# Attention and a Sinkhorn-routed MoE on one core: one plain unit more among the last four, and an earlier clear and cast in the first batch

## The chip, the core and the metric

The kernel runs on one core of one Trainium2 chip. A core has five engines that run their own instruction queues in order: TensorE (PE, matrix products; weight loads are shown apart as PEld), VectorE (DVE), ScalarE (ACT), GpSimd (POOL) and SyncE (SP), and 16 DMA engines that move data between HBM and the on-chip memory. Transfers are issued from the queues of SP, ACT and POOL. The metric is device time in microseconds (us) of one execution; lower is better.

## The reference

The program is an attention layer followed by a mixture of experts.

```python
# attention: 8 batches, 8 heads, 512 local and 32 global tokens, head dim 64
k_all = np.concatenate([k_g, k_l], axis=2); v_all = np.concatenate([v_g, v_l], axis=2)
out_g = np.matmul(sm(scale * q_g @ k_all.T), v_all)          # global queries see all keys
s_ll  = np.where(abs(i - j) <= 32, scale * q_l @ k_l.T, -1e9) # local queries: a band
s_l   = np.concatenate([scale * q_l @ k_g.T, s_ll], axis=-1)  # and all 32 global keys
out_l = np.matmul(sm(s_l), np.concatenate([v_g, v_l], axis=2))
# mixture of experts: x is 4352 tokens x 512, 8 experts, hidden size 1024
P = np.exp(x @ w_gate - max); 8 times: rows and columns of P normalised (Sinkhorn)
for e in range(8):
    out += P[:, e:e+1] * (np.maximum(x @ w1[e], 0) @ w2[e])
```

`sm` is the softmax. All inputs are float32; the kernel computes matrix products in float16 with float32 accumulation.

## The kernel before

**Stages.** From 0 to about 305 us the attention runs, one head pair per step `s` (32 steps, `hp` is the pair within a batch `b`), with matmuls of experts 0 and 1 put between its steps from step 5 on. From about 323 to 352 us the Sinkhorn iterations run, with matmuls of those two experts around and between them. From 357 us to the end experts 2 to 7 run, in two passes over halves of the tokens, by Strassen's scheme with seven products in place of eight: the first layer in slots of 512 columns (`Slot`), the second layer in units of two 128-token tiles (`Unit`). The order of all engines' instructions is the order in which the code writes them; each engine takes its own in that order.

**The first batch.** GpSimd's queue, in the order written, holds: q and k of heads 2 and 3 of batch 0 (`steps[0:2]`), the mask's four selects (L310), q and k of heads 4 to 7 (`steps[2:4]`, L174), then `load_v(0)`. Its `first()` issues `cast_vg(0)` (L183: the global values of the batch, cast to float16 into a scratch tensor in HBM) and the first local load of `va` (L193, 96 rows); three whole loads of `va` (L196) and one of `vb` (L200) follow. Then come `cast_vg(1)` and `clear_z(0)` (L296 to L301). That last function sets the padded tile `vgz` of the global values to zero, writes the column of ones (`own`) and clears the small tile `vgn`. SP's queue has `load_vz(0)` next (L180: four copies from the scratch into every fourth partition of `vgz`) and one copy into `vgn` (L319).

In step 1 GpSimd issues q and k of batch 1 and makes `vb` by copying from `va` (`part`, L204 to L209). `st_E` (L423) multiplies the probabilities with `va`, `vb` and `vgz`; it first runs in step 2. `st_A` (L332) transposes the q and k of a head pair; the pair with heads 4 and 5 is taken in step 1. VectorE's L427 and L428 read what `st_E` wrote.

**A Strassen unit.** `sums` forms three sums of quarters of the hidden activations (and overwrites one quarter) with four `tensor_tensor` operations, L867, on VectorE or on the engine passed to it. Seven products follow, each of four matmuls of 256 columns (L871), into an accumulator `z` of four quarters in PSUM (the pool has two of them): m1, then a copy on ScalarE (L885), m7, m2, m6 with another copy (L892), m4, m5, and m3. VectorE reads the results and adds them, weighted, to the output (L905): `r2` and `r7` after m5, `r1` after m3. In the last expert `r7` and `r1` are followed by a store on SP (L833).

**A plain unit.** `plain` (L931) does the same unit without the scheme: two tiles, each with eight matmuls of 512 columns (L940), in PSUM buffers of their own (pools `ps_mm` and `ps_sc`, two buffers each), read by VectorE at L943. Its argument `between` puts other pieces of work before given matmuls: the key (1, 3) means tile 1, before its matmul 3. With `last` the second tile is cut into 256, 128 and 128 columns. It reads the raw quarters of the activations, so it needs no `sums`.

**The end.** After the last slot (`p`) and the last unit of the regular order (`x`), four units are left, u0 to u3. u0 and u3 are plain, u1 and u2 are Strassen units; u2's sums are formed by GpSimd, and the two units' products are interleaved.

Of the kernel before, what the change touches and what calls it, by code (L numbers as in the profile page):

```python
# [23 lines left out]
def kernel(  # L24
# [13 lines left out]
    nc = tc.nc  # L38
# [14 lines left out]
    FT = F // P  # L53
# [75 lines left out]
    with ExitStack() as att:  # L129
# [22 lines left out]
        def natural(b):  # L152
            return b < 2
# [18 lines left out]
        def load_qk(b, *hs):  # L172
            staged[b] = tuple(att_in.tile([P, H, NJ, Dh], FP16, tag=t, name=t) for t in ("qs", "ks"))
            return [lambda t=t, src=src, h0=h0, h1=h1: nc.gpsimd.dma_start(  # L174
                        out=t[:, h0:h1], in_=src[b, h0:h1].rearrange("h (p s) d -> p h s d", s=NJ))
                    for h0, h1 in zip(hs, hs[1:]) for t, src in zip(staged[b], (q_l, k_l))]

        def load_vz(b):
            for i in range(4):
                nc.sync.dma_start(out=vgz[b % 2][i:P:4, i, :, 0:Dh], in_=vg16[b])  # L180

        def cast_vg(b):
            nc.gpsimd.dma_start(out=vg16[b], in_=v_g[b].rearrange("h g d -> g h d"))  # L183

        def load_v(b):
            va, vb = vab[b % 2]
            vz = vgz[b % 2]
            src = v_l[b].rearrange("h s d -> s h d")

            def first():  # L190
                if b != 1:
                    cast_vg(b)
                nc.gpsimd.dma_start(out=va[W:P, 0, :, 0:Dh], in_=src[0:96])  # L193

            def mid(j):
                nc.gpsimd.dma_start(out=va[:, j, :, 0:Dh], in_=src[P * j - W : P * j + 96])  # L196

            def last():
                r = HB if natural(b) else W
                nc.gpsimd.dma_start(out=vb[r : r + W, NJ - 1, :, 0:Dh], in_=src[Sl - W : Sl])  # L200

            def part(eng, lo):
                if lo:
                    eng.tensor_copy(out=vb[96:P, NJ - 1], in_=va[W : 2 * W, 0])  # L204
                    eng.tensor_copy(out=vb[0:HB, 0:2], in_=va[HB:P, 0:2])
                    eng.tensor_copy(out=vb[0:HB, 2:NJ], in_=va[HB:P, 2:NJ])
                else:
                    eng.tensor_copy(out=vb[HB:P, 0:2], in_=va[0:HB, 1:3])
                    eng.tensor_copy(out=vb[HB:P, 2], in_=va[0:HB, 3])  # L209

            def move():
                if natural(b):
                    return part
                nc.sync.dma_start(out=vb[96:P, NJ - 1], in_=va[W : 2 * W, 0])
                nc.sync.dma_start(out=vb[0:W, :], in_=va[HB : HB + W, :])
                nc.sync.dma_start(out=vb[HB : HB + W, :], in_=va[HB + W : P, :])
                nc.sync.dma_start(out=vb[W:HB, 0 : NJ - 1], in_=va[0:W, 1:NJ])
                nc.sync.dma_start(out=vb[HB + W : P, 0 : NJ - 1], in_=va[W:HB, 1:NJ])
                load_vz(b)

            return [first] + [lambda j=j: mid(j) for j in range(1, NJ)] + [last, move]
# [38 lines left out]
        def run(steps):  # L260
            for f in steps:
                f()
# [14 lines left out]
        steps = load_qk(0, 2, 4, H)  # L277
# [18 lines left out]
        def clear_z(i, eng):  # L296
            eng.memset(vgr[i].bitcast(mybir.dt.uint32), 0)
            eng.tensor_copy(out=vgz[i][:, :, :, Dh], in_=own.unsqueeze(2).to_broadcast([P, 4, H]))
            if i == 0:
                eng.memset(vgn[0 : P - Sg], 0.0)  # L300
                eng.memset(vgn[P - Sg : P, :, Dh:VW], 1.0)  # L301
# [5 lines left out]
        for a in range(2):  # L307
            band = mask[HB * a : HB * (a + 1), 1, 0:KW]
            for base, m, c in ((0, -1, 1), (2 * W, 1, -1)):
                nc.gpsimd.affine_select(out=band, in_=band, compare_op=ALU.is_ge, fill=NEG, base=base,  # L310
                                        pattern=[[c, KW]], channel_multiplier=m)
        run(steps[2:4])
        *steps, move = load_v(0)
        part = move()
        run(steps)
        cast_vg(1)
        clear_z(0, nc.gpsimd)
        load_vz(0)
        nc.sync.dma_start(out=vgn[P - Sg : P, :, 0:Dh], in_=vg16[0])  # L319

        st = {}
# [248 lines left out]
        for s in range(NU + 2):  # L570
            b, hp = divmod(s, HP)
# [189 lines left out]
    with tc.tile_pool(name="tpool", bufs=2) as tpool, \  # L761
# [68 lines left out]
        def store(m, c, eng):  # L830
            if m < B:
                r0 = S * m + Sg + P * c
                eng.dma_start(out=out[r0 : r0 + P, :], in_=ogs[m][:, c, :])  # L833
            else:
                for b in range(4 * c, 4 * c + 4):
                    eng.dma_start(out=out[S * b : S * b + Sg, :], in_=ogs[m][W * (b % 4) : W * (b % 4 + 1), c, :])
# [15 lines left out]
        class Unit:  # L852
# [6 lines left out]
            def o(self, j):  # L859
                return acc_of(self.m)[:, self.c[j], :]  # L860

            def sums(self, eng=nc.vector):
                a11, a12, a21, a22 = self.a
                s = self.s = hsum.tile([P, 3, HF, P], FP16, tag="hs", name="hs")
                for o, x, y, op in ((s[:, 1], a11, a21, ALU.subtract), (a21, a21, a22, ALU.add),
                                    (s[:, 0], a21, a11, ALU.subtract), (s[:, 2], a12, s[:, 0], ALU.subtract)):
                    eng.tensor_tensor(out=o, in0=x, in1=y, op=op)  # L867

            def mm(self, o, lhs, rhs, first):
                for fk in range(HF):  # L870
# [3 lines left out]
            def w(self, i, j):  # L874
                return w2s[self.k][:, HF * i : HF * (i + 1), H2 * j : H2 * (j + 1)]
# [55 lines left out]
        def plain(u, last, between):  # L931
            order = sorted(range(FT), key=lambda fk: (fk % HF == HF - 1, fk))
            for j in range(2):
                for d0, d1 in ((0, H2), (H2, 3 * P), (3 * P, D)) if last and j else ((0, D),):
                    pool, tag = (ps_sc, "sc") if (j + (d0 > 0)) % 2 else (ps_mm, "mm")
                    z = pool.tile([P, D], FP32, tag=tag, name="zp")
                    for n, fk in enumerate(order):
                        for f in between.get((j, n), ()) if d0 == 0 else ():
                            f()
                        nc.tensor.matmul(z[:, d0:d1], u.a[2 * j + fk // HF][:, fk % HF, :], work["last"][:, fk, d0:d1],  # L940
                                         start=(n == 0), stop=(n == FT - 1), skip_group_check=True)
                    o = u.o(j)[:, d0:d1]
                    nc.vector.scalar_tensor_tensor(out=o, in0=z[:, d0:d1], scalar=u.p[j], in1=o, op0=ALU.mult, op1=ALU.add)  # L943
                store(u.m, u.c[j], nc.sync)
# [171 lines left out]
        p, x = state["slot"], state["unit"]  # L1116
        for w in (x.m4, x.m5, x.r2, x.r7, p.m4, p.m3):
            w()
        u0, u1, u2, u3 = final
        u1.sums()  # L1120
        plain(u0, False, {(0, FT - 2): (x.m3, x.r1, lambda: u2.sums(nc.gpsimd)), (1, 3): (u1.m1,)})
        for w in (u1.m7, u1.m2, u1.m6, u2.m1, u1.m4, u1.m5, u1.r2, u1.r7, u2.m7, u2.m2, u2.m6, u1.m3, u1.r1):
            w()
        plain(u3, True, {(0, 3): (u2.m4, u2.m5, u2.r2, u2.r7), (0, FT - 2): (u2.m3, u2.r1)})


# [28 lines left out]
```

## Time and profile before

| | |
|---|---|
| median of 3 runs | 996.84 us (996.23 to 996.92) |
| profiled execution | 996.39 us, of which the span from the first to the last instruction is 994.6 |
| granted TensorE clock, mean | 0.998 |
| busy: PE, DVE, ACT, POOL | 98%, 78%, 66%, 31% of the span |
| HBM read, written | 144.46 MB, 39.58 MB |

The profile is of one execution. A row gives the start and the length in us, the engine, the line of the code, the operation and the tiles (written <- read). What stands in brackets is the idle time of the engine just before and what ended it. A row with a `q` behind the engine's name (SPq) is that of its queue. Rows of groups give the number of instructions (x4), the busy time in us, the mean of one in ns, and the idle time before them with what ended it. "The chain of waits" follows the work that ended last back to the start: at each step to what released it, or to the instruction before it on its engine. Matmuls are pipelined: the next starts before the last one's end, so two starts lie closer than one is long.

### The profile page before, as it was taken

The numbers are of one execution on the slowest core, as the hardware profiler recorded it, in microseconds if no ns is written. First come the engines' busy times: TensorE is split into PE (matmuls) and PEld (weight loads), VectorE is DVE, ScalarE is ACT, GpSimd is POOL, SyncE is SP. The second block draws the span as 40 slices with busy tenths as digits, with TensorE's granted clock in tenths as the row PEclk, the third lists the DMA queues.
The fourth block names the chain that finished last, engine by engine and source line by source line (L and its number), as shares of the span: only waits on it lengthen the run. The fifth ranks groups of instructions, "written<-read, shape, count | busy, mean of one in ns | idle before, by whom it ended". The sixth has DMA issues, their size and how long they took to land.

```text
span 994.6 us, 22109 instructions
## 1 busy us (share of the span) xinstructions
PE 978.8 (98%) x8644; PEld 637.0 (64%) x8644; DVE 776.9 (78%) x1919; ACT 659.8 (66%) x1372; POOL 305.2 (31%) x366
## 2 busy tenths in 40 slices
PE   7899999999999999999999999999999999999997
PEld 5565556555555556666666666676767676766765
DVE  7876666666663755899999888997899999888887
ACT  6898888888884566765555555557765555555551
POOL 9649887887860201111111111101111111100001
PEclk9999999999999999999999999999999999999999
DMA  9999999999952477554443333575654543123043
GB/s 165 189 163 207 226 213 212 224 203 234 225 141 85 121 229 189 161 138 118 117 106 75 75 74 75 138 212 138 160 138 118 117 116 71 38 56 73 2 106 128
DMA packets 138248, 138.65 MB, mean 139 GB/s; under 512 B 56800, under 2 KB 110240, under 8 KB 136096
## 3 DMA queue, kind: packets, MB, share of 16 engines
q0 software_dynamic: 105696, 87.32, 51.6%
q1 hardware_dynamic: 31888, 49.60, 15.7%
q8 instruction: 67, 1.10, 0.4%
q10 hardware_dynamic: 560, 0.33, 0.1%
q14 instruction: 37, 0.30, 0.1%
HBM read 144.46 MB, written 39.58 MB: 185 GB/s over the span
## 4 chain that ended last, share of the span: by engine, by line
PE 93%; DVE 2%; ACT 2%; POOL 1%; DMA 1%; issue 1%; SPq 0%; ACTq 0%; DVEq 0%; POOLq 0%
PE z L871 30%; PE pa L969 18%; PE py L537 12%; PE ph L523 11%; PE pb L969 9%; PE pc L969 4%; PE sc L375 1%; PE po L423 1%; PE ptw L389 1%; ACT Pu L382 1%; PE pk L332 1%; DMA vgz<-vg 1%; PE tgx L399 1%; PE pq L332 1%; PE sg L455 0%
## 5 line engine op out<-in xcount | busy, mean ns | idle before, releaser
L871 PEld LDWEIGHTS <-hs 128*128 128x128 f16 x2320 | 226.1, 98 | 96.1 <-issue 2.9
L871 PE MATMUL z<-w2e,hs 128*128 128x256 f16 x1336 | 200.4, 273 | 2.3 <-DVE o L905 1.0
L871 PE MATMUL z<-v,hs 128*128 128x256 f16 x984 | 147.6, 273 | 0.0
L892 ACT COPY z<-z 128x256 f32<-128x256 f32 x100 | 35.7, 357 | 145.9 <-PE z L871 145.9
L523 PE MATMUL ph<-xT,w1e 128*128 128x512 f16 (+1 forms) x576 | 130.2, 367 | 0.6 <-ACT xT L407 0.6
L537 PE MATMUL py<-w2e,hT 128*128 128x512 f16 x544 | 128.2, 379 | 0.0
L382 ACT ACTIVATE Pu<-ms,mx 128x160 f16<-128x160 f32 x256 | 119.6, 637 | 11.7 <-DVE mx L379 9.6
L969 PEld LDWEIGHTS <-w1e 128*128 128x128 f16 x960 | 87.1, 98 | 51.6 <-issue 1.0
L969 PE MATMUL pa<-t,s 128*128 128x512 f16 x384 | 114.2, 379 | 0.0
L787 POOL DMA_DIRECT2D w1e<-in_moe_w_dram x24 | 17.4, 733 | 290.7 <-PE pa L969 220.4
L379 DVE CUSTOM_DVE_ANT_0 ms<-sc,mask 128x160 f32<-128x160 f32 x256 | 70.0, 320 | 46.3 <-ACT yst L540 27.6
L867 DVE TENSOR_TENSOR hs<-hs 128x512 f16<-128x512 f16 x228 | 99.1, 435 | 8.4
L905 DVE SCALAR_TENSOR_TENSOR oy<-z,lg,oy 128x512 f32<-128x512 f32 x128 | 95.8, 748 | 7.3 <-ACT oy L910 5.9
L787 POOL DMA_DIRECT2D w2e<-in_moe_w_dram x24 | 19.8, 830 | 243.6 <-PE z L871 214.2
L973 DVE CUSTOM_DVE_ANT_0 hx<-pb,s 128x512 f16<-128x512 f32 x96 | 65.9, 686 | 36.4 <-ACT s L1003 30.4
L523 PEld LDWEIGHTS <-w1e 128*128 128x128 f16 x576 | 54.5, 98 | 53.0 <-issue 1.1
L989 ACT ACTIVATE hs<-pa 128x512 f16<-128x512 f32 x96 | 57.2, 596 | 46.8 <-PE pa L969 46.8
L973 DVE CUSTOM_DVE_ANT_0 hs<-pb,s 128x512 f16<-128x512 f32 x96 | 65.8, 686 | 24.1 <-ACT s L1003 23.7
L969 PEld LDWEIGHTS <-s 128*128 128x128 f16 x720 | 65.6, 98 | 28.5 <-issue 0.3
L537 PEld LDWEIGHTS <-hT 128*128 128x128 f16 x544 | 49.9, 98 | 51.9
L528 DVE TENSOR_SCALAR hT<-ph 128x512 f16<-128x512 f32 x58 | 40.1, 691 | 50.1 <-PE ph L523 50.0
L526 ACT ACTIVATE hT<-ph 128x512 f16<-128x512 f32 (+1 forms) x86 | 50.7, 589 | 27.6 <-PE ph L523 27.1
(203 smaller groups left out, 1935.0 us busy)
## 6 DMA issues: line engine op xcount, KB each, us to landing
ys<-yd SPq DMA_DIRECT2D x68, 256.0 KB, 3.2
yd<-yst SPq DMA_DIRECT2D x16, 1024.0 KB, 6.4
pw<-in_moe_w_dram POOLq DMA_DIRECT2D x24, 512.0 KB, 10.1
kept<-psum POOLq DMA_DIRECT2D x24, 512.0 KB, 4.8
s<-kept POOLq DMA_DIRECT2D x12, 768.0 KB, 8.8
v<-kept POOLq DMA_DIRECT2D x12, 768.0 KB, 8.7
w1e<-in_moe_w_dram POOLq DMA_DIRECT2D x12, 512.0 KB, 5.4
w2e<-in_moe_w_dram POOLq DMA_DIRECT2D x12, 512.0 KB, 6.5
```

What stands on the lines that cost most here:

```text
L379: nc.vector.tensor_tensor_reduce(out=ms[:, ii, :], in0=sc[:, SW * ii : SW * (ii + 1)], in1=mask[:, mi, :], scale=-scale, scalar=BIG, op0=A ...
L382: nc.scalar.activation(out=d["Pu"][:, i // 4, :, i % 4], in_=ms[:, ii, :], func=AF.Exp, scale=-1.0, bias=d["mx"][:, i : i + 1])
L523: nc.tensor.matmul(ph[:, 0:n], wts[e][0][:, dk, P * fm : P * (fm + 1)], xT[:, dk, c0 : c0 + n], start=(dk == 0), stop=(dk == DP - 1))
L526: nc.scalar.activation(out=hT[:, fm, 0:n], in_=ph[:, 0:n], func=AF.Relu)
L528: nc.vector.tensor_scalar(out=hT[:, fm, 0:n], in0=ph[:, 0:n], scalar1=0.0, scalar2=None, op0=ALU.max)
L537: nc.tensor.matmul(py, hT[:, fk, P * c : P * (c + 1)], wts[e][1][:, fk, :], start=(fk == 0), stop=(fk == FT - 1))
L867: eng.tensor_tensor(out=o, in0=x, in1=y, op=op)
L871: nc.tensor.matmul(o, lhs[:, fk, :], rhs[:, fk, :], start=(first and fk == 0), stop=(fk == HF - 1), skip_group_check=True)
L905: nc.vector.scalar_tensor_tensor(out=o, in0=z, scalar=p, in1=o, op0=ALU.mult, op1=ALU.add)
L969: nc.tensor.matmul(o, lhs[:, dk, P * f : P * (f + 1)], rhs[:, dk], start=(first and n == 0 and dk == 0), stop=(dk == HD - 1), skip_group_c ...
L973: nc.vector._custom_dve(TENSOR_ADD_SAT, out=self.to(i, j), in0=self.of(ps), in1=self.of(s), s0=BIG, s1=0.0)
L989: nc.scalar.activation(out=self.to(1, 0), in_=self.of(self.pa), func=AF.Relu)
```

## The change

Two places. At the start the cast of the first batch's global values, `cast_vg(0)`, is issued ahead of the second q/k pair (`steps[2:4]`) instead of inside `first()`; `clear_z(0)` stands behind the first local load instead of behind all loads and `cast_vg(1)`; and `load_vz(0)` is written behind the loads, ahead of `cast_vg(1)`. At the end u2 becomes a plain unit. It no longer has sums (`sums` loses its argument for the engine), u1's later products and reads stand between u2's matmuls, and u3 has nothing between its own.

```diff
             def first():
-                if b != 1:
+                if b > 1:
                     cast_vg(b)
                 nc.gpsimd.dma_start(out=va[W:P, 0, :, 0:Dh], in_=src[0:96])
...
+        cast_vg(0)
         run(steps[2:4])
         *steps, move = load_v(0)
         part = move()
-        run(steps)
+        steps[0]()
+        clear_z(0, nc.gpsimd)
+        run(steps[1:])
+        load_vz(0)
         cast_vg(1)
-        clear_z(0, nc.gpsimd)
-        load_vz(0)
         nc.sync.dma_start(out=vgn[P - Sg : P, :, 0:Dh], in_=vg16[0])
...
-            def sums(self, eng=nc.vector):
+            def sums(self):
...
-                    eng.tensor_tensor(out=o, in0=x, in1=y, op=op)
+                    nc.vector.tensor_tensor(out=o, in0=x, in1=y, op=op)
...
         u1.sums()
-        plain(u0, False, {(0, FT - 2): (x.m3, x.r1, lambda: u2.sums(nc.gpsimd)), (1, 3): (u1.m1,)})
-        for w in (u1.m7, u1.m2, u1.m6, u2.m1, u1.m4, u1.m5, u1.r2, u1.r7, u2.m7, u2.m2, u2.m6, u1.m3, u1.r1):
+        plain(u0, False, {(0, FT - 2): (x.m3, x.r1), (1, 3): (u1.m1,)})
+        for w in (u1.m7, u1.m2, u1.m6):
             w()
-        plain(u3, True, {(0, 3): (u2.m4, u2.m5, u2.r2, u2.r7), (0, FT - 2): (u2.m3, u2.r1)})
+        plain(u2, False, {(0, 3): (u1.m4, u1.m5, u1.r2, u1.r7), (1, 3): (u1.m3, u1.r1)})
+        plain(u3, True, {})
```

## The prediction

> **What bounds the kernel now.** First the page, for the engine on which the chain of waits ends.
>
> ```profile
> PE 93%; DVE 2%; ACT 2%; POOL 1%; DMA 1%; issue 1%; SPq 0%; ACTq 0%; DVEq 0%; POOLq 0%
> ```
>
> TensorE (PE) holds 93% of the chain, so the middle of the kernel has no room. What can be won lies where the chain leaves PE: in the first 22 us and the last 20. There I read the chain piece by piece (start, length, what). At the start:
>
> ```profile
> 11.27 0.97 POOL vgz L297
> 13.31 0.60 SPq L180
> 13.96 0.61 SPq L180
> 14.61 6.71 DMA vgz<-vg
> ```
>
> GpSimd (POOL) issues all its loads, only then clears the padded tile (from L297 on); SP then issues four copies into it, one after another, and the fourth lands at 14.61 + 6.71 = 21.32. PE's rows in order of time say what that costs:
>
> ```profile
> 20.53 0.19 PE L423 MATMUL po<-vgz,pg 128*64 128x65 f16 x1
> 21.36 0.19 PE L423 MATMUL po<-vgz,pg 128*64 128x65 f16 x1 [0.64 <-DMA vgz<-vg]
> ```
>
> Between the two starts lie 0.83 us, and without the wait some 0.03: a stall of 0.8. Now the end: the longest pieces of the chain, then the groups of the last 21 us.
>
> ```profile
> 980.95 0.67 DVE oy L905
> ...
> 983.96 0.76 DVE ox L905
> ...
> 987.70 0.76 DVE o L905
> ```
>
> ```profile
> L871 PE MATMUL z<-w2e,hs 128*128 128x256 f16 x36 | 5.4, 272 | 2.3 <-DVE o L905 1.0 <-DVE oy L905 1.0 <-DVE ox L905 0.3
> L867 POOL TENSOR_TENSOR hs<-hs 128x512 f16<-128x512 f16 x4 | 4.8, 1196 | 29.5 <-DVE hs L867 29.2
> L867 DVE TENSOR_TENSOR hs<-hs 128x512 f16<-128x512 f16 x4 | 4.3, 1070 | 0.2
> ```
>
> PE waits three times for VectorE (DVE): 1.0, 0.3 and 1.0 us. First: u2's m1 needs the accumulator that x.r1 empties (the piece at 980.95), and x.r1 stands in VectorE's queue behind u1's four sums, which take 1070 ns each while GpSimd forms u2's. Second and third: m3 of u1 goes on when r7 of u1 has ended (983.96 + 0.76 = 984.72), m3 of u2 when r7 of u2 has (988.46). With two Strassen units side by side there is too little other PE work between a unit's m5 and its m3.
>
> **The change, part one: the end.** On PE u2's 28 matmuls of 256 columns go and 16 of 512 come. Prices from unbroken pieces of the chain:
>
> ```profile
> 971.27 1.31 PE z L871 x12
> ...
> 985.36 0.65 PE zp L940 x3
> ```
>
> 28 x 1.31 / 12 = 3.06 us against 16 x 0.65 / 3 = 3.47: PE gets 0.41 more work.
>
> The waits that go: 2.3 us idle in the group's row above. Each restart also lays bare the tail of the matmul before it (272 ns long, started 109 apart: 0.16), three times 0.16 = 0.49. Together 2.8.
>
> What is late next? I lay the new order on the old clock. Up to u1.m6 PE's order is the old one. m6's last matmul ends at about 980.7 (the copy below starts on it), so PE's next turn is 0.16 earlier, 980.54. Then: three matmuls of plain(u2), to 981.19; m4 and m5 of u1, 0.44 each, to 982.06; eight of plain(u2), to 983.78; m3; five more, to 985.30; plain(u3). m4 writes what ScalarE's copy after m6 reads:
>
> ```profile
> 980.73 0.36 ACT L892 COPY z<-z 128x256 f32<-128x256 f32 x1 [2.03 <-PE z L871]
> ```
>
> That ends at 981.09, 0.1 ahead of m4's turn. r2 can begin some 0.2 us after m5 (its matmuls' tail and the semaphore), 982.26; r2 and r7 take 0.76 each and 0.03 between them, to about 983.80, so m3, due at 983.78, may wait 0.07. VectorE gets there in time, because the sums alone take
>
> ```profile
> L867 DVE TENSOR_TENSOR hs<-hs x1: 426/426/426, 971.7 to 971.7; 128x512 f16<-128x512 f16 x1
> ```
>
> 0.43 each: begun at 976.5 they end near 978.3, x.r1 and plain(u0)'s two reads follow by 980.5, and the rest (r2, r7, r1, three reads of 0.75, three shorter ones) is 5.7 us of work for 9 us of PE. The sums that GpSimd loses (4.8 us) are made by nobody else: a plain unit needs none. The stores move with the reads. Net: -2.76 + 0.41 + 0.07 = **-2.3 us**. Bounds: -2.4 (no new wait) and -1.3 (one wait of 1.0, as the longest of the three, comes back). I take -2.3, since every due time lies within 0.1 of free.
>
> **Part two: the start.** GpSimd's queue as it is (the rows left out between 11 and 13 are the rest of the clear, L298 to L301):
>
> ```profile
> 5.13 0.75 POOL L174 DMA_DIRECT2D ks<-in_k_l_dram  x1
> 5.86 0.66 POOL L183 DMA_DIRECT2D vg<-in_v_g_dram  x1
> 6.51 0.79 POOL L193 DMA_DIRECT2D va<-in_v_l_dram  x1
> 7.29 2.65 POOL L196 DMA_DIRECT2D va<-in_v_l_dram  x3
> ...
> 11.27 0.96 POOL L297 MEMSET vgz<- 128x1040 uint32 x1
> ...
> 13.15 0.78 POOL L174 DMA_DIRECT2D qs<-in_q_l_dram  x1
> ...
> 17.86 1.05 POOL L206 COPY vb<-va 64x1040 f16<-64x1040 f16 x1
> ...
> 19.96 0.61 POOL L209 COPY vb<-va 64x520 f16<-64x520 f16 x1
> ```
>
> The clear takes 13.15 - 11.27 = 1.9 us and moves ahead of the x3 row, to 7.3; the cast of v_g (0.65) moves two places forward. Nothing is added, so from 13.15 on GpSimd stands where it stood. The tile and its copy of `own` are ready at 8.7. v_g, issued at 4.4, lands by 11.4 even at the 7.0 us of the k load below; so SP's first copy starts between 8.7 and 11.4, the fourth 2.0 later, and at today's 6.7 lands between 17.4 and 20.1: before PE asks at 20.7. The 0.8 goes. The page gives transfers 1% of the chain in all, and the four copies' 6.7 us are that share: nothing behind 21.4 waits for a load, so what is gained here should reach the end.
>
> What becomes late instead is what is pushed back: the second q/k pair by 0.65 us, the whole local loads and the one after them by 1.9, each queue behind. Landings (issue to landing) of the k load and of the third whole local load, and the rate of the queues from 11 to 13.9:
>
> ```profile
> ks<-in_k_l_dram POOLq DMA_DIRECT2D x1, 256.0 KB, 7.0
> ```
>
> ```profile
> va<-in_v_l_dram POOLq DMA_DIRECT2D x1, 128.0 KB, 7.0
> ```
>
> ```profile
> DMA packets 3403, 0.43 MB, mean 148 GB/s; under 512 B 3395, under 2 KB 3403, under 8 KB 3403
> ```
>
> The third local load is issued at 9.05 (the last third of the x3 row) and lands at 16.05; its first reader is L206 at 17.86: 1.8 us of room. If landings are set by the backlog of bytes, the later issue costs nothing, and only the four copies go ahead: 4 x 32 KB at 148 GB/s, 0.9: 16.9, no wait. If they are set by the issue, 1.9 + 0.9: 18.9, L206 waits 1.0, and L209 ends at 21.6 where PE wants it at 20.7: 0.1 worse than the stall of today. The k load lands at 5.13 + 7.0 = 12.1 and is first read here:
>
> ```profile
> 13.01 0.64 PE L332 MATMUL pk<-identity,ks 128*64 128x128 f16 x8
> ```
>
> With the issue 0.65 later and a share of the copies ahead it lands between 12.4 and 13.2: 0 to 0.2 us of wait. Of 7.0 us to landing only 0.75 is issue, which is nearest to the backlog case; I take -0.8 + 0.15 = **-0.6**, bounds -0.8 and +0.3 (late local values, late keys).
>
> The Trainium skill ("DMA: Bandwidth & Descriptors", section "Queues, rings and completion order") states that a DMA engine serves the rows that have work in turn, packet by packet. By that rule SP's copies would not wait behind GpSimd's backlog but cut into it, and the k load is the one they hit; an estimate from the copies' share puts that at the upper end, 0.2. No row here shows it for these copies, which now run later.
>
> **Sum.** -2.3 - 0.6 = -2.9 against the profiled execution's 996.39 (span 994.6 and 1.8 around it): 993.5. The median of the runs is 996.84, 0.45 above that execution: **993.9**.
>
> **Rivals.**
> *The start gives nothing.* The issue sets the landing; L206 waits, or PE waits at 13.01. For it: the moved work, 1.9 us, is as long as the room, 1.8. Against: the backlog. 996.84 - 2.3 + 0 to 0.3: 994.5 to 994.8.
> *The end gives half.* One wait of 1.0 comes back, m4 behind ScalarE's copy or m3 behind r7, whose room is 0.1 and nothing. 994.9; with the start lost too, 995.5.
> *No change.* The waits are not u2's: PE stands as before in u1's m4 and m3, pays 0.41 for the wider matmuls and wins 0.6 at the start: 996.6. Against: the first and third wait are u2's own m1 and m3, which no longer exist.
> *Slower.* Late local values at L206: every microsecond past 18.0 adds one to the end. It eats the gain of the end and the start when the third load lands at 18.0 + 0.8 + 2.3 = 21.1, 5 us later than now; 2 us beyond that, at 23.1, the kernel takes 998.9. The worst sum above is 18.9.
>
> **How the numbers follow.** 0.2%, 2.0 us, is about what a measurement of this kernel can tell from no change. Chances: forecast 0.70 (993.3 to 994.4), start lost 0.16, end halved 0.08, no change 0.04, slower 0.02. Faster by over 0.2%, that is under 994.85: 0.70 + 0.16 and a little of the third, 0.87; within it 0.10; slower 0.03. Range: low 996.84 - 2.4 - 0.8 less the runs' spread of 0.6, 993.0; high the third case, 995.0.
>
> **What would show it.** Right: the row at 21.36 has lost its wait; the start's chain holds no vgz; PE's waits on L905 in the last 20 us fall from 2.3 to about 0.1; L867 on GpSimd is gone and on VectorE takes 0.43. Wrong: L206 starts later than 17.9; PE stands at L332 near 13; L871 waits for L905 or L892 near the end.

## The result, and the profile after

| | before | after |
|---|---|---|
| median | 997.0 us (996.23 to 999.38, 11 runs) | 994.66 us (994.44 to 995.75, 11 runs) |
| ratio after to before | | 0.9974, 95% interval 0.9966 to 0.9983 |
| profiled execution, its span | 996.39 us, 994.6 | 994.72 us, 992.9 |

By the ratio the change makes the kernel 0.26% faster: 2.6 us of 997.0, with an interval from 1.7 to 3.4; the two medians lie 2.3 us apart. 993.9 was forecast. To see where the time came from I split the span at the first matmul of u0. Both traces have it in PE's rows in order of time, first before, then after:

```profile
974.90 1.46 PE L940 MATMUL zp<-w2e,hs 128*128 128x512 f16 x6
```

```profile
975.52 1.46 PE L942 MATMUL zp<-w2e,hs 128*128 128x512 f16 x6
```

From there to the end of the span: 994.6 - 974.90 = 19.7 before, 992.9 - 975.52 = 17.4 after. The end gives 2.3 us. Everything ahead of it became 975.52 - 974.90 = 0.6 us *longer*, though the forecast had the start 0.6 shorter.

**The end after.** The groups from 972 us on (count, busy us, mean ns of one, then the idle time before them):

```profile
L942 PE MATMUL zp<-w2e,hs 128*128 128x512 f16 (+2 forms) x64 | 11.4, 326 | 0.0
...
L873 PE MATMUL z<-w2e,hs 128*128 128x256 f16 x24 | 3.6, 272 | 0.0
...
L869 DVE TENSOR_TENSOR hs<-hs 128x512 f16<-128x512 f16 x5 | 2.1, 425 | 0.2
```

PE's group of 256 columns, which carried 2.3 us of waits, has 0.0. A sum on VectorE takes 425 ns, where it took 1070 beside GpSimd's. The places where a new wait could come, in PE's and VectorE's rows:

```profile
982.68 1.89 PE L942 MATMUL zp<-w2e,hs 128*128 128x512 f16 x8
984.47 0.60 PE L873 MATMUL z<-w2e,hs 128*128 128x256 f16 x4
```

```profile
977.11 1.87 DVE L869 TENSOR_TENSOR hs<-hs 128x512 f16<-128x512 f16 x4
...
982.88 1.54 DVE L907 SCALAR_TENSOR_TENSOR ox<-z,lg,ox 128x512 f32<-128x512 f32 x2 [1.92 <-PE z L873]
```

Eight matmuls of 512 columns start 0.217 apart (0.65 for three), 1.73; m3 of u1 starts 1.79 behind the first of them. The wait for r7 is 0.06; the forecast had 0.07. VectorE is 1.92 us idle before r2, so it isn't the bound.

**The start after.** The view of who waited for `vgz` names no engine any more, and the chain of waits runs through the compute engines without a transfer. The share of PE on the whole chain rises from 93% to

```profile
PE 95%; ACT 3%; DVE 1%; issue 0%; DVEq 0%; ACTq 0%
```

but the band product `st_E` of step 0 (call it E(0)) comes later, not sooner. Its first and last rows before:

```profile
20.35 0.22 PE L423 MATMUL po<-va,pw 128*64 128x65 f16 x1
...
21.67 0.20 PE L423 MATMUL po<-vgz,pg 128*64 128x65 f16 x2
```

The same after, with GpSimd's L206:

```profile
18.43 1.05 POOL L206 COPY vb<-va 64x1040 f16<-64x1040 f16 x1 [0.54 <-DMA va<-in_v_l_dram]
21.73 0.22 PE L425 MATMUL po<-va,pw 128*64 128x65 f16 x1
22.23 0.20 PE L425 MATMUL po<-vgz,pg 128*64 128x65 f16 x2
```

With the stall the last row was at 21.67. No wait stands in front of E(0) now; PE simply arrives 1.4 us later. Some 0.35 us of that are there early: PE takes the global keys (`kgs`, L249) at 6.43 before and at 6.78 after. The windows of 2 us show where the rest comes from. The third number from the right is the granted TensorE clock (0.91 in the first row), ahead of the share and the rate of the DMA. Before, then after:

```profile
14.00:16.00 2.00, 2.00 (x41) 1.24 (x39) 1.24 (x5) 1.31 (x4) 2.00 (x3) 0.91 1.85 109
16.00:18.00 2.00, 1.69 (x34) 1.18 (x27) 1.97 (x11) 2.00 (x6) 1.90 (x4) 1.00 1.59 191
```

```profile
14.00:16.00 2.00, 2.00 (x17) 1.00 (x14) 1.01 (x5) 1.87 (x5) 2.00 (x3) 0.50 3.19 118
16.00:18.00 2.00, 2.00 (x43) 1.59 (x40) 1.40 (x8) 0.61 (x2) 1.79 (x3) 0.70 1.92 161
```

Each execution has a stretch at half the clock in the start. A mean of 0.91 over 2 us means that it ended 2 x 2 x (1 - 0.91) = 0.36 us into the window, at 14.4; a mean of 0.70 in the next window puts the end at 17.2 in the execution after. The same three matmuls show it as lengths, 0.99 us before and 1.46 after:

```profile
14.00 0.99 PE L553 MATMUL pm<-kTe,identity 128*128 128x512 f16 x3
```

```profile
14.56 1.46 PE L555 MATMUL pm<-kTe,identity 128*128 128x512 f16 x3
```

Whether the change or the execution decides on that clock is the question for the experiments.

### The profile page after: what moved, and what is told of

Same layout as the page of the kernel before. It is cut to its first block, busy times and chain, and to the rows that moved or that the text cites. A ratio compares the mean times of both kernels' runs of the same rounds, so it can differ in the third digit from the quotient of the medians.

```text
span 992.9 us, 22075 instructions
## 1 busy us (share of the span) xinstructions
PE 980.8 (99%) x8632; PEld 636.9 (64%) x8632; DVE 773.9 (78%) x1918; ACT 659.5 (66%) x1370; POOL 300.6 (30%) x362
## 4 chain that ended last, share of the span: by engine, by line
PE 95%; ACT 3%; DVE 1%; issue 0%; DVEq 0%; ACTq 0%
PE z L873 31%; PE pa L971 18%; PE py L539 12%; PE ph L525 11%; PE pb L971 9%; PE pc L971 4%; PE ptw L391 1%; ACT Pu L384 1%; PE po L425 1%; PE sc L377 1%; PE zp L942 1%; PE pk L334 1%; PE tgx L401 1%; PE pq L334 1%; DVE ms L381 0%; PE sg L457 0%
## 5 line engine op out<-in xcount | busy, mean ns | idle before, releaser
L873 PEld LDWEIGHTS <-hs 128*128 128x128 f16 x2292 | 223.4, 98 | 93.1 <-DVE hs L869 0.7
L873 PE MATMUL z<-w2e,hs 128*128 128x256 f16 x1320 | 198.0, 273 | 0.0
L539 PE MATMUL py<-w2e,hT 128*128 128x512 f16 x544 | 128.2, 379 | 0.0
L789 POOL DMA_DIRECT2D w1e<-in_moe_w_dram x24 | 17.4, 733 | 295.4 <-PE pa L971 220.4
L869 DVE TENSOR_TENSOR hs<-hs 128x512 f16<-128x512 f16 x228 | 96.6, 424 | 8.4
L539 PEld LDWEIGHTS <-hT 128*128 128x128 f16 x544 | 49.9, 98 | 52.0
```

The source lines that it names most:

```text
L539: nc.tensor.matmul(py, hT[:, fk, P * c : P * (c + 1)], wts[e][1][:, fk, :], start=(fk == 0), stop=(fk == FT - 1))
L869: nc.vector.tensor_tensor(out=o, in0=x, in1=y, op=op)
L873: nc.tensor.matmul(o, lhs[:, fk, :], rhs[:, fk, :], start=(first and fk == 0), stop=(fk == HF - 1), skip_group_check=True)
```

## Experiments

**The two parts alone.** The end's part in the kernel before:

```diff
-        plain(u0, False, {(0, FT - 2): (x.m3, x.r1, lambda: u2.sums(nc.gpsimd)), (1, 3): (u1.m1,)})
...
+        plain(u2, False, {(0, 3): (u1.m4, u1.m5, u1.r2, u1.r7), (1, 3): (u1.m3, u1.r1)})
+        plain(u3, True, {})
```

> The kernel before with the end of the change alone: u2 plain, no sums on GpSimd; the start is the old one. Theory A (the end is worth what the two profiles show from plain(u0)'s first matmul to the last instruction: 994.6 - 974.9 = 19.7 us before, 992.9 - 975.5 = 17.4 after): 2.3 us faster than before, 994.5 to 994.8, ratio 0.9977, and the row of E(0)'s wait for vgz (0.64 before) is still there. Rival: part of the 2.3 us measured for the whole change is due to the start; then this kernel gains clearly less than 2.3.

Measured: 994.57 us (994.33 to 997.45, 8 runs), ratio 0.9974 (0.9964 to 0.9984), and 17.4 us from u0 to the end. The end's part alone gives all that the whole change gives. The row of E(0)'s wait for `vgz`, which was expected to be there still, is not: in this execution PE came at 21.72, and `vgz` landed at 21.75.

The start's part in the kernel before:

```diff
+        cast_vg(0)
         run(steps[2:4])
...
+        steps[0]()
+        clear_z(0, nc.gpsimd)
+        run(steps[1:])
```

> The kernel before with the start of the change alone: cast and clear early; the end is the old one. In the profile after, the first scores' chain came 0.6 us later behind the start, not 0.8 earlier, and TensorE was granted half its clock for 6.83 us from 10.4 on, against 3.41 us from 11.0 before. Theory A (that loss is the clock's phase, which differs from execution to execution, and late loads take 0.5 of the 0.8 as well: L206 waited 0.54 us): the median is 0 to 0.6 faster than before, and the profile shows another pattern of granted clock than the one after, with the start late or early accordingly. Theory B (the early clear itself makes the start 0.6 slower, always): 0.5 to 0.7 slower than before, in a profile with any pattern of clock.

Measured: 997.06 us (996.27 to 998.35, 11 runs), ratio 0.9996 (0.9987 to 1.0005), that is -0.4 us with an interval from -1.3 to +0.5, which holds both the -0.6 of the forecast and nothing. The stall at `vgz` is gone here too, but another took its place. Its GpSimd and PE rows, and the piece of the chain in front of L206:

```profile
10.93 8.50 DMA va<-in_v_l_dram
```

```profile
19.48 1.05 POOL L206 COPY vb<-va 64x1040 f16<-64x1040 f16 x1 [1.57 <-DMA va<-in_v_l_dram]
20.89 0.22 PE L425 MATMUL po<-va,pw 128*64 128x65 f16 x1
21.68 0.19 PE L425 MATMUL po<-vb,pw 128*64 128x65 f16 x1 [0.58 <-POOL vb L208]
22.46 0.20 PE L425 MATMUL po<-vgz,pg 128*64 128x65 f16 x2
```

The third whole local load takes 8.50 us from issue to landing (7.0 in the profile of before), L206 waits 1.57 us for it, and PE waits 0.58 for `vb`. That is the case behind the prediction's upper bound for the start, which had L206 wait 1.0.

**The clear behind the local loads.** In the changed kernel; the cast stays early:

```diff
-        steps[0]()
+        run(steps[:4])
         clear_z(0, nc.gpsimd)
-        run(steps[1:])
+        run(steps[4:])
```

> The changed kernel with clear_z(0) moved behind the three whole local loads (the early cast stays, as does the end). The local loads are then issued 1.9 us earlier than in the changed kernel, as in the kernel before but for the cast. Theory A (late local loads hold GpSimd at L206 for 0.54 us and so take the gain of the start): L206 waits for nothing, SP's fourth copy still lands before 20, and the time is 0.2 to 0.5 below the changed kernel's, 994.2 to 994.5. Theory B (the copies into the tile, not the loads, decide): the copies start 2.7 us later, near 12, land near 19, and nothing changes or it is slower.

Measured: 994.65 us (994.33 to 995.05, 6 runs), ratio 0.9967 (0.9956 to 0.9979). L206 has no wait any more and starts at 17.81, as in the kernel before. So the early clear is what makes the local loads late. But the time is that of the changed kernel (994.66) all the same, not the 994.2 to 994.5 expected: in these two profiles the late loads cost nothing, because PE comes to E(0) at 21.60 and 21.73.

**A shorter half clock.** Five matmuls more that nobody reads, ahead of `cast_g("qgs")` in step 0, in the changed kernel:

```diff
+                keep_busy(5)
```

> The changed kernel with five matmuls of 512 columns, which nobody reads, put on TensorE behind the last scores of step 0, where it stands idle for 1.3 us at 9.7 to 11.1. Theory A (TensorE's clock falls to half at 10.4 because it was idle too much in the stretch before): the stretch at half clock in the start is shorter than 6.83 us or gone, the executions lie closer together, and the median is 0.3 to 1.4 below the changed kernel's. Theory B (the half clock comes from the phase of a window that no work of the kernel moves): the same pattern, and the five matmuls (1.1 us at full clock, 2.1 at half) make the start up to 0.8 slower.

Measured: 994.98 us (994.21 to 996.98, 11 runs), ratio 0.9977 (0.9968 to 0.9986). The half clock ended at 13.3, but the five matmuls ran inside it,

```profile
10.57 2.32 PE L555 MATMUL pm<-kTe,identity 128*128 128x512 f16 x5
```

for 2.32 us, and E(0) began at 22.22, later than anywhere else. This profile doesn't price the filler, though. PE had already stood 1.08 us for VectorE's `kgs`, until 7.54 (6.78 in the changed kernel), because the load of the global keys was late; that lies ahead of the filler and isn't its doing. Nor does one execution show that the filler shortened the half clock: it lasted 3.4 us in before too, without any. The runs show no gain, and they lie further apart than the changed kernel's (994.44 to 995.75), so the expected 0.3 to 1.4 below didn't come. What filler at other places would give wasn't tried.

**The end taken apart.** Kernel before, with u2's sums on VectorE instead of GpSimd:

```diff
-        plain(u0, False, {(0, FT - 2): (x.m3, x.r1, lambda: u2.sums(nc.gpsimd)), (1, 3): (u1.m1,)})
+        plain(u0, False, {(0, FT - 2): (x.m3, x.r1, u2.sums), (1, 3): (u1.m1,)})
```

> The kernel before with one word changed: u2's sums are formed by VectorE, behind x.r1, not by GpSimd. Both units stay Strassen units and interleaved. Measure: from plain(u0)'s first matmul to the last instruction, 19.7 us before, 17.4 with the change. Theory A (the two causes add: the sums slowed by GpSimd cost the first wait, 1.1 us; the interleaving costs the two waits of m3): u1's sums take 0.43 each, the first wait goes, m3's waits stay, and the stretch is 18.6 to 18.9. Theory B (GpSimd's sums are the whole cause): 17.4 less the 0.4 that the narrow matmuls save, 17.0 to 17.3. Theory C (they cost nothing): 19.5 to 19.8.

Measured: one run, 996.41 us; from u0 (975.89) to the end of the span (994.6) 18.7 us, against 19.7. Of the group's three waits one is gone:

```profile
L871 PE MATMUL z<-w2e,hs 128*128 128x256 f16 x40 | 6.0, 272 | 1.3 <-DVE o L905 1.0 <-DVE ox L905 0.3
```

The wait of 1.0 for `oy` is the price of forming the sums on two engines at once. So the three waits were not one thing: 1.0 us belonged to the sums' place, 1.3 to the order of the products.

All of the last four units plain, in the changed kernel:

```diff
+        plain(u0, False, {(0, FT - 2): (x.m3, x.r1)})
+        plain(u1, False, {})
+        plain(u2, False, {})
```

> The changed kernel with u1 plain as well, so that all of the last four units are plain and no sums are formed behind the last slot. Measure: the stretch from plain(u0)'s first matmul to the last instruction, 17.42 us with the change. Theory A (PE's work alone decides once the waits are gone: a plain unit is 0.41 dearer than a Strassen unit, and m3's wait of 0.07 goes): 17.7 to 17.8. Rival (waits are still hidden in the changed kernel's end): 17.4 or less.

Measured: one run, 995.24 us, 993.5 - 975.70 = 17.8 us from u0. PE goes through without a break,

```profile
977.43 12.72 PE L942 MATMUL zp<-w2e,hs 128*128 128x512 f16 x74
```

and pays some 0.3 us more than with u1 by Strassen's scheme. That fits the prediction's 0.41 for wider matmuls less the wait of m3: a plain unit is dearer, and it pays only as long as it covers waits.

Both units by Strassen's scheme, but in another order, with the sums on VectorE (and the start of the clear behind the local loads):

```diff
+        plain(u0, False, {(0, FT - 2): (x.m3, x.r1, u2.sums), (1, 3): (u1.m1,)})
+        for w in (u1.m7, u1.m2, u1.m6, u2.m1, u1.m4, u1.m5, u1.r2, u1.r7, u2.m7, u2.m2, u2.m6):
...
+        plain(u3, True, {(0, 3): (u1.m3, u2.m4, u2.m5, u1.r1, u2.r2, u2.r7), (1, FT - 1): (u2.m3, u2.r1)})
```

> The kernel with the clear behind the three whole local loads, and an end of another order: u1 and u2 both by Strassen's scheme, both sums on VectorE, u2's m7, m2 and m6 and three matmuls of plain(u3) between u1's m5 and m3, and u2's m3 ahead of the last 256-column matmul of plain(u3). Theory A (the scheme loses nothing by itself, only by what stands between m5 and m3): the stretch from plain(u0)'s first matmul to the end is 17.1 to 17.4, 0.1 to 0.3 below the change's 17.42, and the time is 994.3 to 994.6, as fast as the changed kernel within what can be measured. Theory B (two Strassen units in the last four always leave waits): 18 us or more.

Measured: 994.48 us (993.8 to 994.87, 10 runs), ratio 0.9974 (0.9965 to 0.9984); 992.3 - 974.86 = 17.4 us from u0, as with u2 plain. No PE wait is left:

```profile
L873 PE MATMUL z<-w2e,hs 128*128 128x256 f16 x38 | 5.8, 273 | 0.0
```

PE has the 0.41 us less work, and the end doesn't get it: the chain's last pieces are now VectorE's, where u2's r1 stands ahead of u3's last reads.

```profile
987.73 0.75 DVE o L907
988.48 0.39 DVE o L945
988.87 0.26 DVEq L1152
989.12 0.26 DVE o L945
```

So it wasn't Strassen's scheme for u2 that cost 2.3 us, but where its sums were formed and in what order the products stood. Making u2 plain is one way of covering the waits, a new order another that is worth as much.

**The kernel before once more, and the start's parts again.** Without an edit, for the clock in the start:

> The kernel before, once more, for another execution of its start. In the profile of before TensorE ran at half clock for 3.41 us and E(0) waited 0.64 us for vgz; with the old start and the new end half clock lasted 6.83 us and E(0) came at 21.7, behind vgz. Theory A (whether the wait exists depends on how long the half clock lasts in that execution): with 3.41 us of half clock E(0) starts near 20.4 and waits again, with 6.83 near 21.7 and doesn't. Theory B (the wait is there in every execution): it waits 0.5 or more with either. The stretch at the end is 19.7 again.

One run, 996.99 us. Its half clock ended at 15.0 instead of 14.4, and the stall is there again. Theory A missed: the half clock lasted 6.8 us here (from 8.1), and yet E(0) began at 20.73 and waited. What the arrival follows is when the half clock ends, not how long it lasts.

```profile
14.00:16.00 2.00, 2.00 (x33) 1.10 (x29) 1.07 (x4) 1.53 (x5) 2.00 (x4) 0.76 1.68 88
```

```profile
20.73 0.22 PE L423 MATMUL po<-va,pw 128*64 128x65 f16 x1
21.86 0.19 PE L423 MATMUL po<-vgz,pg 128*64 128x65 f16 x1 [0.75 <-DMA vgz<-vg]
22.17 0.20 PE L423 MATMUL po<-vgz,pg 128*64 128x65 f16 x2
```

Next the start with the clear behind the local loads, and the old end; the edit is that of the kernel above, in the kernel with the start's part alone.

> The end as before; at the start the cast of v_g goes ahead of the second q/k pair, and the clear goes behind all three whole local loads, ahead of the load of vb. Theory A (the end of the first band product is the latest of three: the compute chain, whose arrival follows the end of the half-clock stretch; the landing of vgz; and GpSimd's copies into vb): no wait for vgz, L206 starts by 18.0, and PE does not wait for vb. At a half clock that ends near 15 us the band product of E(0) ends 0.4 to 0.7 us sooner than in the kernel before at the same phase (22.17 at 15.0); at one that ends past 16.4 there is no difference. The median is 0.0 to 0.7 us below before, near 0.3. Theory B (the start's change has a gain of its own, whatever the clock): 0.6 to 0.8 below before. Theory C (it costs): above before.

Measured: 996.71 us (996.11 to 997.55, 11 runs), ratio 0.9993 (0.9984 to 1.0002), -0.7 us with an interval from -1.6 to +0.2, which doesn't exclude nothing. L206 starts at 17.79, and nothing waits for `vgz` or `vb`. Then one run each of two kernels again:

> The kernel of start_only a second time. Theory A: L206 waits again for a whole local load and starts past 18.2; if the half clock ends before 15.5, PE waits again for vb at L425; if it ends past 16.4, PE comes at 21.6 or later and does not wait. Theory B: L206's wait is an accident of one execution: it starts by 18.0.

> The changed kernel a second time. Theory A: no wait for vgz at L425; L206 waits and starts past 18.2; the stretch from u0's first zp matmul to the end is 17.4; the band product of E(0) ends between 22.1 and 22.5 whatever the clock's phase. Theory B: with an early end of the half clock it ends near 21.6.

997.15 and 994.90 us. L206 waits again, 0.61 and 1.36 us, and starts at 18.53 and 19.23; PE comes to E(0) at 21.90 and 21.92 and doesn't wait. E(0)'s last row is at 22.40 and 22.42.

All executions with one of the three starts, by the end of the half clock (worked out from the windows as above; two traces lack the record, but have the three matmuls of L555 at the long 1.46). The last column is E(0)'s last row, from which what follows keeps its distance: the first matmul into `py` (L537, or L539 after the change) starts 37.7 to 37.8 us behind it in each of them, and the first matmul of u0 953.2 to 953.4. So this column is what the start is worth to the whole.

| start | kernel | half clock ends | E(0) begins | `vgz` landed | PE waits | E(0)'s last row |
|---|---|---|---|---|---|---|
| before | before | 14.4 | 20.35 | 21.32 | 0.64, `vgz` | 21.7 |
| before | before once more | 15.0 | 20.73 | 21.82 | 0.75, `vgz` | 22.2 |
| before | sums on VectorE | 16.6 | 21.63 | 22.28 | 0.31, `vgz` | 22.6 |
| before | end alone | 16.6 | 21.72 | 21.75 | none | 22.2 |
| changed | start alone | 14.9 | 20.89 | 18.51 | 0.58, `vb` | 22.5 |
| changed | start alone, again | 17.1 | 21.90 | 17.58 | none | 22.4 |
| changed | after | 17.2 | 21.73 | 17.58 | none | 22.2 |
| changed | after, again | no record | 21.92 | 18.81 | none | 22.4 |
| changed | all plain | no record | 21.87 | 15.78 | none | 22.4 |
| clear behind the loads | both reordered | 15.3 | 21.07 | 18.31 | none | 21.6 |
| clear behind the loads | that start, old end | 16.2 | 21.48 | 19.18 | none | 22.0 |
| clear behind the loads | with the new end | 16.5 | 21.60 | 18.18 | none | 22.1 |

Three things can be last ahead of E(0): the compute chain, whose arrival goes with the end of the half clock, whatever the kernel; the landing of `vgz`; and the copies into `vb`. The changed start takes `vgz` out of the race in all five executions, and in the one whose half clock ended early `vb` came in. The last column is 22.2 on average with the old start, 22.4 with the changed one and 21.9 with the clear behind the loads; four of the five executions of the changed start have a late clock, so these averages aren't at equal clock. At nearly the same clock, 14.9 to 15.3, with one execution of each, it is 22.2, 22.5 and 21.6. Past 16.4 the old start's last row is at 22.2 or 22.6, against 22.1 to 22.4 for the others, which arrive with the chain. Nothing here makes the clock the change's doing: its half clock ends anywhere from 14.4 to 16.6 with the old start and from 14.9 to 17.2 with the changed one. These few executions couldn't show a small effect.

## Why the prediction was right at the end and wrong at the start

**The end, -2.3: right, term by term.** The waits of 2.3 are 0.0; m3's new wait was 0.06 against 0.07; m4 didn't wait for ScalarE; the sums took 425 ns against the 0.43 taken from the row of one; the wider matmuls' price is borne out by the run with all units plain. 19.7 to 17.4 is -2.3.

**The start, -0.6: wrong, and this is the step that failed.** What came is the first rival, "the start gives nothing", given 0.16: 994.5 to 994.8. The forecast itself had 993.3 to 994.4; that the time still lies inside the whole range, 993.0 to 995.0, is owed to the end alone. By 997.0 - 2.3 the end's part alone makes 994.7. The run's interval, -1.7 to -3.4, would have room for -2.9, and that of the start alone for -0.6; it is the rows that decide, and by the last column of the table the changed start brings E(0) no sooner. The mechanism at `vgz` was right: SP's fourth copy landed at 17.6, inside the 17.4 to 20.1 given (15.8 to 18.8 in the five executions), and the row at 21.36 has lost its wait. Two of its terms were mis-sized.

*-0.8 for the stall.* It was read from one execution as if it belonged to the code. In four executions of the old start PE waited 0.64, 0.75, 0.31 us and not at all, because both members of the race move: the compute chain reaches E(0) between 20.35 and 21.72, later the later the half clock ends, and `vgz` lands between 21.32 and 22.28. "Before PE asks at 20.7" and "the 0.8 goes" hold only for a half clock that ends near 14.4, and the profiled execution of before had the earliest end in the table. Its windows have a granted clock of 0.74 and 0.50 from 10 to 14 us; the prediction looked at the rate of the queues there and not at the clock.

The Trainium skill ("TensorE: Matmul & The Clock Gate", section "Part 1: The HAM clock gate") states that the clock is set by windows of 3413 ns that run freely and don't start with the kernel, so that the moment of change differs from run to run. The trace agrees: the half clock lasted 3.4 us in before (11.0 to 14.4) and 6.8 in after (10.4 to 17.2), one and two such windows, at another place in each execution.

*+0.15 for late loads.* The keys weren't late: PE's L334 had no wait at 13.56. But the local values were. I chose the backlog ("of 7.0 us to landing only 0.75 is issue") and 16.9 for the third load; it landed just ahead of L206, at 18.3 to 19.4 in the five executions of the changed start, on both sides of the upper bound of 18.9. Issue to landing didn't shrink when the issue was moved back by 1.9 us: it is 7.4 to 8.5 us there, against 7.0 to 8.3 in the four executions of the old start. On average the landing moved from 16.7 to 18.7, by about what the issue moved. So the landing follows the issue, and the backlog was the wrong choice. With the clear behind those loads it is all gone, and L206 starts at 17.8.

The Trainium skill ("DMA: Bandwidth & Descriptors", section "Queues, rings and completion order") has a DMA engine serve the queues with work in turn, so that SP's copies would cut into GpSimd's loads. No run here shows them doing so: the k load landed at 12.1 to 12.7 in the five executions and at 12.2 to 12.4 with the old start, and the third local load's time to landing differs by no more than it does between executions of one start.

The late local values didn't reach the end in the profile after only because the chain was late too. "Against: the backlog" was no row, but a choice between two readings of one. So the rival's number came partly by luck: its cause, a wait for late local values, reached PE in one execution of five, and in the others it was the later arrival of the chain that left nothing to win.

**The rivals.** "The end gives half" and "no change" didn't come: no wait came back. "Slower" by late local values at L206 is the right mechanism at a small price: 0.58 us at PE in one execution of the start alone, none in four others.

## What to carry to other kernels

A stall in one profile is the gap between two arrivals; before its removal is booked, ask what sets the other one, and look at the granted clock in the windows ahead of it: here a second profile of the same code moved it by 1.0 us (20.89 and 21.90 with the start alone). Work that is moved ahead of loads costs the loads their place in the queue; keep the loads that are read first in front, as in the three executions with the clear behind them, where nothing at E(0) waited. Where PE waits at the end, try the order and the engine of the small operations before the arithmetic is made dearer; both gave the same 2.3 us here.

## What the runs showed of the hardware

- In the start the half clock lasted 3.4 or 6.8 us and ended between 14.4 and 17.2 in executions of the same or nearly the same code without filler; the arrival at E(0) followed at about half that shift, from 20.35 to 21.9.
- GpSimd's issue of a transfer can itself wait for an earlier one to land. In the second execution of before the chain holds the first row below, and GpSimd's L183, eight issues behind that load, is idle for 0.63 us until it has landed; that moves the clear and all four copies, and `vgz` lands at 21.82 instead of 21.32. The same wait, 0.55 and 0.87 us, is in the two other executions of the old start, and L183 starts some 0.3 us behind the landing in all three. In the first execution of before the load landed at 10.13, ahead of L183's turn at 10.64, and there was no wait. Whether the queue or a semaphore of the program holds the issue isn't shown.

```profile
4.37 6.53 DMA qs<-in_q_l_dram
```

```profile
11.18 0.59 POOL L183 DMA_DIRECT2D vg<-in_v_g_dram  x1 [0.63 <-DMA qs<-in_q_l_dram]
```

- Sums of two tiles on VectorE took 1070 ns each while GpSimd formed others, and 425 alone; on GpSimd 1196. Two engines side by side were no faster than VectorE by itself: eight sums in 976.93 + 5.02 - 976.49 = 5.5 us by the rows of before below (VectorE, GpSimd), against 1.87 + 1.79 on VectorE alone in the kernel with the sums there.

```profile
976.49 4.45 DVE L867 TENSOR_TENSOR hs<-hs 128x512 f16<-128x512 f16 x4
```

```profile
976.93 5.02 POOL L867 TENSOR_TENSOR hs<-hs 128x512 f16<-128x512 f16 x4 [29.22 <-DVE hs L867]
```
